# A fused conv–joint forward and backward kernel: first-chunk tanh rows by DMA transpose, SyncE's queue in source order, and the second chunk's x tiles moved up

## The chip, the cores and the metric

The kernel runs on one core of a Trainium2 chip. The metric is the device time of one execution in microseconds (us); lower is better. The kernel before took 866.32 us in the median of three runs (863.22 to 870.09).

## What is computed

The reference is the forward pass below and its gradients to all seven inputs for a given `grad_out`, all in bf16. B = 2, T = 16000, D = 256, three taps, U = 8.

```python
def _fwd_reference(x, w1, w2, g, w_f, w_g, w_o):
    h = sum over 3 taps of xp[:, i:i+T, :] @ w1[i]      # conv over time
    h = gelu(h)[:, ::2, :]                               # stride 2
    f = sum over 3 taps of hp[:, i:i+T1, :] @ w2[i]
    f = gelu(f)[:, ::2, :]                               # stride 2: 4000 rows
    fe = f @ w_f
    ge = g @ w_g
    j = tanh(fe[:, :, None, :] + ge[:, None, :, :])      # [2, 4000, 8, 256]
    return j @ w_o
```

The outputs are the result `out_0` [2, 4000, 8, 256] and the gradients of x, w1, w2, g, w_f, w_g and w_o. The bulk of the data is `grad_out` (read) and `out_0` (written).

## The kernel before

**Tiling.** The 4000 output rows of each batch are cut into 8 chunks of 512 rows (the last has 416), so there are 16 chunks, numbered n = 0 to 15. In a chunk the 8 values of u are taken in 4 pairs `up`. One pair is one *step*: a gradient part `gj` (L529), forward blocks `o_block` (L629), and the weight gradient `gwo` (L675) of the pair before.

**What runs beside what.** The main loop (L773) runs the pairs of chunk n (`joint_units`, L613, cut into short units by `yield`) and, woven between them by `weave` (L692), a *fill*: the convolutions of chunk n+1 (`conv_units` L227, `conv2_units` L264, `fe_units` L293), and the backward convolutions of chunk n−1. `ratio` (L800) is the number of fill units per main unit. Chunk 0 has no chunk before it, so its fill holds only the convolutions of chunk 1 and six empty units. The gelu pieces are queued and issued by `pump` (L194), one or two per main unit.

**x, grad_out and tanh tiles.** `load_x` (L130) brings one of four phases of x transposed into a tile XC (6 buffers) by a DMA transpose, `load_got` (L141) brings `grad_out` transposed (GOT, 6 buffers), `load_go` (L147) brings it as rows (GO, 3 buffers). The last chunk of each batch has 32 rows over; for these `load_go` brings four small pieces (GOs, 1 buffer, L158). All are issued on SyncE's queue (SP).

**JR: the tanh rows.** `tanh` (L307) writes JT with the channel on the partitions. The weight gradient `gwo` needs the same values with the row on the partitions, the tile JR (3 buffers). For n > 0, `load_jr` (L563) makes them by four DMA transposes per pair on SP (L574), issued in `ahead` (L811), after the tanh of the next pair. For n == 0 `load_jr` returns after it has allocated the tile (L569), and `joint_units` calls `jr_block` for each of the four 128-row blocks (L622–625): four transposes on TensorE into PSUM (L392) and one VectorE copy out of PSUM (L394).

**What sets the order.** The program is written in one order, but the framework's scheduler orders each engine's instructions itself: the source's order is a priority, and an instruction that the scheduler's own timing takes to be ready goes ahead. This holds for SP's queue also. Each queue is then executed in the order so fixed. Weights W2, WF, WO are loaded on SP at L709–711. The first loads after those are written at L760–766: two GOT, GO of pair 0, two GOT, and then the four x tiles of chunk 1. In each step (L801–809) the source loads one x tile of chunk n+2, GO of the next pair and two GOT tiles; then come the units of the pair, with `ahead` among them.

Of the kernel before, what the change touches and what calls it, by code (L numbers as in the profile page):

```python
# [22 lines left out]
P = 128  # L23
# [9 lines left out]
def kernel(  # L33
# [22 lines left out]
    nc = tc.nc  # L56
# [4 lines left out]
    G = len(chunks)  # L61
    xq = x.rearrange("b (q four) d -> b four q d", four=4)

    def geom(n):
        b, ci = chunks[n]
        c0 = ci * CW
        return b, ci, c0, min(CW, MQ - c0)

    def blocks(w):
        return [(o, min(P, w - o)) for o in range(0, w, P)]  # L70
# [59 lines left out]
    def load_x(n, c):  # L130
        b, ci, c0, W = geom(n)
        t = xcp.tile([P, KT, CW + 16], BF16, name="XC")
        if c == 3 and ci > 0:
            nc.sync.dma_start_transpose(out=t[:, :, 0:W + 16], in_=xq[b, c, c0 - 16:c0 + W, :])
        else:
            if c == 3:
                nc.vector.memset(t[:, :, 0:16], 0.0)
            nc.sync.dma_start_transpose(out=t[:, :, 16:16 + W], in_=xq[b, c, c0:c0 + W, :])
        S[n]["X", c] = t

    def load_got(n, u):  # L141
        b, ci, c0, W = geom(n)
        t = gotp.tile([P, KT, CW], BF16, name="GOT")
        nc.sync.dma_start_transpose(out=t[:, :, 0:W], in_=grad_out[b, c0:c0 + W, u, :])
        S[n]["GOT", u] = t

    def load_go(n, up):  # L147
        b, ci, c0, W = geom(n)
        t = gop.tile([P, 4, 2 * V], BF16, name="GO")
        nfull = W // P  # L150
        src = grad_out[b, c0:c0 + nfull * P, 2 * up:2 * up + 2, :]
        nc.sync.dma_start(out=t[:, 0:nfull, :], in_=src.rearrange("(tb p) u v -> p tb (u v)", p=P))
        S[n]["GO", up] = t
        r = W - nfull * P
        if r and up % 2 == 0:
            t = tailp.tile([P, V], BF16, name="GOs")
            for i in range(4):
                nc.sync.dma_start(out=t[i * r:(i + 1) * r, :], in_=grad_out[b, c0 + nfull * P:c0 + W, 2 * up + i, :])  # L158
            S[n]["GOs", up // 2] = t


# [367 lines left out]
    def gj(n, u):  # L529
        b, ci, c0, W = geom(n)  # L530
        st = S[n]
        JT, GOT = st["JT", u], st["GOT", u]
        JSQ = jsp.tile([P, KT, CW], BF16, name="JSQ")
        nc.scalar.activation(out=JSQ[:, :, :W], in_=JT[:, :, :W], func=ACT.Square)  # L534
        NGZ = ngzp.tile([P, KT, CW], BF16, name="NGZ")
        st["NGZ", u] = NGZ
        for mt in range(KT):
            ps = ps_f32()
            for kt in range(KT):
                nc.tensor.matmul(ps[:, :W], lhsT=WOT[:, kt, mt * P:(mt + 1) * P], rhs=GOT[:, kt, :W],  # L540
                                 start=(kt == 0), stop=(kt == KT - 1))
            nc.vector.scalar_tensor_tensor(out=NGZ[:, mt, :W], in0=JSQ[:, mt, :W], scalar=1.0, in1=ps[:, :W],  # L542
                                           op0=ALU.subtract, op1=ALU.mult,
                                           accum_out=NGGEc[:, b, mt, u, ci:ci + 1])
            yield
# [17 lines left out]
    def load_jr(n, up):  # L563

        W = geom(n)[3]
        nfull = W // P
        JR = jrp.tile([P, 4, 2, KT, P], BF16, name="JR")
        S[n]["JR", up] = JR
        if n == 0:  # L569
            return  # L570
        for j in range(2):
            JT = S[n]["JT", 2 * up + j]
            for kt in range(KT):
                nc.sync.dma_start_transpose(out=JR[:, 0:nfull, j, kt, :], in_=JT[:, kt, 0:nfull * P])  # L574
# [38 lines left out]
    def joint_units(n, up, ahead):  # L613
        b, ci, c0, W = geom(n)
        st = S[n]
        bl = blocks(W)[:W // P]
        us = (2 * up, 2 * up + 1)
        for u in us:
            yield from gj(n, u)
            ngfe_acc(n, u)  # L620
            short_jt(n, u)
        if n == 0:  # L622
            for k in range(len(bl)):
                jr_block(n, up, k)
                yield
        OUT = outp.tile([P, 4, 2 * V], BF16, name="OUT")
        JR = st["JR", up]

        def o_block(k):  # L629
            o, M = bl[k]  # L630
            ps = ps_f32()
            for j, u in enumerate(us):
                for kt in range(KT):
                    nc.tensor.matmul(ps[:M, j * V:(j + 1) * V], lhsT=st["JT", u][:, kt, o:o + M], rhs=WO[:, kt, :],  # L634
                                     start=(kt == 0), stop=(kt == KT - 1))
            nc.scalar.copy(out=OUT[:M, k, :], in_=ps[:M, :])  # L636

        ahead()
        pend = prev_gwo[0]
        o_block(0)  # L640
        yield
        o_block(1)
        yield
        if pend is not None:
            gwo(*pend, 0)
        yield
        if pend is not None:
            gwo(*pend, 1)
        yield
        for k in range(2, len(bl)):  # L650
            o_block(k)
            yield
            if pend is not None:
                gwo(*pend, k)
        yield
        if pend is not None:
            gwo_rest(*pend, len(bl))
        yield
        if W % P and up % 2:
            yield from short_block(n, up // 2)  # L660
        prev_gwo[0] = (n, up)
        nfull = W // P
        nc.gpsimd.dma_start(out=out_0[b, c0:c0 + nfull * P, us[0]:us[1] + 1, :].rearrange("(tb p) u v -> p tb (u v)", p=P),  # L663
                            in_=OUT[:, 0:nfull, :])
# [27 lines left out]
    def weave(main, fill, ratio):  # L692

        due = 0.0
        for _ in main:
            pump(2 if later else 1)
            due += ratio
            while due >= 1.0:
                due -= 1.0
                if next(fill, StopIteration) is StopIteration:  # L700
                    due = -1e9

    make_identity(nc, ident[:])
    nc.gpsimd.dma_start(out=W1[:], in_=w1.rearrange("i (kt p) n -> p i kt n", p=P))
    for c in (1, 0, 3, 2):
# [53 lines left out]

    for i in range(2):  # L760
        load_got(*order[i])
    load_go(*orderp[0])
    for i in range(2, 4):
        load_got(*order[i])
    for c in (1, 0, 3, 2):
        load_x(1, c)
    for _ in chain(warm(16), small_units(), conv_units(0), transposed_units(), warm(4), conv2_units(0), warm(16), fe_units(0)):
        pass
    for u in range(2):
# [3 lines left out]
    for n in range(G):  # L773
        back, fwd = n > 0, n + 1 < G
        conv = conv_units(n + 1) if fwd else iter(())
        parts = []
        if back:
            for (o, M) in blocks(window(n - 1)[1] - window(n - 1)[0]):
                load_x5(n - 1, o, M)
            d1, e, gwf = d1_units(n - 1), e_units(n - 1), gwf_units(n - 1)  # L780
            nfn = (len(blocks(geom(n - 1)[3])) + 1) // 2
            d5, gw2 = d5_units(n - 1), gw2_units(n - 1)
            nhg = len(blocks(geom(n - 1)[3]))
            parts += [islice(conv, 2), islice(d1, 1), islice(conv, 1), d1, conv,
                      islice(gwf, 1), islice(d5, 1), islice(gwf, nfn - 1), islice(d5, 1), islice(gw2, 1),
                      islice(d5, 1), islice(gw2, 1), d5, islice(gw2, nhg - 2), gwf, gw2]
        else:
            parts += [conv, iter([None] * 3)]
        if fwd:
            parts.append(conv2_units(n + 1))  # L790
        if back:
            parts.append(islice(e, 6))
        else:
            parts.append(iter([None] * 3))
        if fwd:
            parts.append(fe_units(n + 1))
        if back:
            parts.append(e)
        fill = chain(*parts)
        ratio = (0.85 if n > 0 else 0.28) if n + 1 < G else 0.72  # L800
        for up in range(U // 2):  # L801
            step = n * (U // 2) + up
            if n + 2 < G:
                load_x(n + 2, (1, 0, 3, 2)[up])
            if step + 1 < len(orderp):
                load_go(*orderp[step + 1])
            for i in range(2):
                if 2 * step + 4 + i < len(order):
                    load_got(*order[2 * step + 4 + i])

            def ahead():  # L811
                for i in range(2):
                    if 2 * step + 2 + i < len(order):
                        tanh(*order[2 * step + 2 + i])
                if step + 1 < len(orderp):
                    load_jr(*orderp[step + 1])

            weave(joint_units(n, up, ahead), fill, ratio)
            if up == U // 2 - 1:
                for _ in fill:  # L820
                    pump(2)
                pump(len(later) + len(lazy))
                lazy_on[0] = False
# [35 lines left out]
    n = G - 1  # L859
# [35 lines left out]
```

## Time and profile before

| what | us |
|---|---|
| median of 3 runs | 866.32 |
| the profiled execution, its own time | 865.56 |
| its span in the profile | 863.8 |
| TensorE (PE) busy | 831.3 |
| ScalarE (ACT) busy | 684.2 |
| VectorE (DVE) busy | 602.2 |
| GpSimd (POOL) busy | 407.2 |

The granted TensorE clock of this execution is 0.997 of full. PE's busy time includes overlap between pipelined matmuls. SP does no arithmetic; it only issues DMAs. A row of a table by windows gives a stretch of the span, its length, and the busy time of each engine in it; "x16" is a number of instructions. In the chain of waits each piece has its start, its length and what it was. "A <- B" names a wait of A that ended with B.

### The profile page before, as it was taken

How to read it: one execution, taken by the hardware profiler on the slowest of the kernel's cores; microseconds unless marked ns; L12 is line 12 of the kernel's file. 1: busy time of each engine (PE TensorE's matmuls, PEld its weight loads, DVE VectorE, ACT ScalarE, POOL GpSimd, SP SyncE). 2: the span in 40 equal slices, each digit the busy share in tenths (PEclk: the TensorE clock that was granted, in tenths of full speed). 3: DMA queues.
4: the chain of work that ended last, by engine and by line, in shares of the span. 5: the costliest groups of instructions: out<-in, count | busy, mean ns of one | idle time of the engine just before them, and what ended most of it. 6: DMA issues, size and time to landing. Idle time of an engine off the chain costs nothing.

```text
span 863.8 us, 17772 instructions
## 1 busy us (share of the span) xinstructions
PE 831.3 (96%) x6648; PEld 599.3 (69%) x6648; DVE 602.2 (70%) x1190; ACT 684.2 (79%) x1064; POOL 407.2 (47%) x452
## 2 busy tenths in 40 slices
PE   7878999999999999999999999999999999999998
PEld 3455777767767677777856677776776767777876
DVE  4697958759495784949678495875948669495552
ACT  4788897886969869696996969879696886969634
POOL 1255554535544444554453554543553535545750
PEclk9999999999999999999999999999999999999999
DMA  9999999999999999999899999999999999997952
GB/s 188 188 198 187 174 239 224 222 266 203 259 226 224 206 222 252 199 226 246 192 212 218 219 218 231 234 224 265 192 249 229 221 259 184 223 223 180 225 160 90
DMA packets 382612, 185.66 MB, mean 215 GB/s; under 512 B 330114, under 2 KB 366235, under 8 KB 382526
## 3 DMA queue, kind: packets, MB, share of 16 engines
q1 hardware_dynamic: 362878, 115.20, 76.7%
q0 software_dynamic: 19648, 69.32, 26.6%
q8 instruction: 52, 0.85, 0.4%
q14 instruction: 34, 0.28, 0.2%
HBM read 54.43 MB, written 50.34 MB: 121 GB/s over the span
## 4 chain that ended last, share of the span: by engine, by line
PE 53%; DVE 29%; ACT 13%; issue 2%; DMA 2%; POOL 0%; ACTq 0%; POOLq 0%; DVEq 0%
PE ps L512 8%; PE GWO_ps L683 7%; PE ps L246 7%; PE ps L489 7%; PE ps L540 7%; PE ps L634 6%; DVE NGZ L542 6%; DVE G L199 5%; DVE g_sq L199 5%; DVE g_s L197 4%; DVE GH L381 3%; PE pst L392 3%; ACT JSQ L534 3%; PE ps L378 3%; ACT JT L312 2%
## 5 line engine op out<-in xcount | busy, mean ns | idle before, releaser
L561 POOL TENSOR_TENSOR ACCN<-ACCN,NGZ 128x1024 f32<-128x1024 f32 (+1 forms) x80 | 170.3, 2129 | 126.6 <-DVE NGZ L542 124.1
L542 DVE SCALAR_TENSOR_TENSOR NGZ<-JSQ,ps 128x512 bf16<-128x512 bf16 (+1 forms) x256 | 163.4, 669 | 83.6 <-ACT GX L492 47.7
L534 ACT ACTIVATE JSQ<-JT 128x1024 bf16<-128x1024 bf16 (+1 forms) x128 | 135.3, 1061 | 86.6 <-DVE NGZ L542 86.6
L312 ACT ACTIVATE JT<-FE,GE 128x512 bf16<-128x512 f32 (+1 forms) x256 | 171.2, 737 | 0.1
L636 ACT CAST OUT<-ps 128x512 bf16<-128x512 f32 x248 | 147.7, 614 | 3.8 <-PE ps L634 3.3
L634 PE MATMUL ps<-WO,JT 128*128 128x256 bf16 x992 | 148.1, 272 | 0.9 <-DVE NGZ L542 0.5
L683 PE MATMUL GWO_ps<-GO,JR 128*128 128x256 bf16 x992 | 140.2, 273 | 0.0
L540 PE MATMUL ps<-GOT,WOT 128*128 128x512 bf16 (+1 forms) x512 | 138.4, 374 | 1.8 <-DVE JR L394 1.1
L197 DVE SCALAR_TENSOR_TENSOR g_s<-g_sq,g_x 128x1024 bf16<-128x1024 bf16 (+1 forms) x45 | 74.7, 1659 | 58.5 <-ACT g_sq L197 58.5
L634 PEld LDWEIGHTS <-JT 128*128 128x128 bf16 x992 | 94.5, 98 | 24.9 <-issue 1.4
L683 PEld LDWEIGHTS <-JR 128*128 128x128 bf16 x992 | 95.3, 98 | 18.3 <-issue 1.1
L489 PE MATMUL ps<-W1T,GH 128*128 128x256 bf16 (+2 forms) x768 | 104.2, 273 | 0.0
L512 PE MATMUL ps<-rows,X 128*128 128x256 bf16 (+2 forms) x768 | 94.2, 272 | 8.1 <-DVE rows L394 8.1
L331 DVE TENSOR_TENSOR ACC<-ACC,ps 128x512 f32<-128x512 f32 x84 | 55.4, 680 | 57.4 <-PE ps L512 56.3
L246 PE MATMUL ps<-XC,W 128*128 128x512 bf16 (+1 forms) x384 | 91.9, 376 | 2.7 <-DMA XC<-in_x_dram 2.4
L512 PEld LDWEIGHTS <-X 128*128 128x128 bf16 (+2 forms) x768 | 74.5, 98 | 23.1 <-issue 11.5
L663 POOL DMA_DIRECT2D out_dram<-OUT x64 | 49.4, 772 | 86.8 <-ACT OUT L636 84.4
L492 ACT CAST GX<-ps 128x512 bf16<-128x512 f32 (+2 forms) x128 | 74.3, 592 | 15.0 <-PE ps L489 11.6
L489 PEld LDWEIGHTS <-GH 128*128 128x128 bf16 (+2 forms) x768 | 75.0, 99 | 15.6 <-issue 1.4
L540 PEld LDWEIGHTS <-WOT 128*128 128x128 bf16 x512 | 49.1, 98 | 43.9 <-issue 2.6
L502 POOL DMA_DIRECT2D out_dram<-GX x60 | 33.6, 559 | 70.1 <-ACT GX L492 64.1
L246 PEld LDWEIGHTS <-W 128*128 128x128 bf16 x384 | 37.7, 98 | 40.7 <-issue 4.4
(139 smaller groups left out, 1289.3 us busy)
## 6 DMA issues: line engine op xcount, KB each, us to landing
GO<-in_grad_out_dram SPq DMA_DIRECT2D x56, 512.0 KB, 5.2
out_dram<-OUT POOLq DMA_DIRECT2D x56, 512.0 KB, 5.4
X<-in_x_dram POOLq DMA_DIRECT2D x58, 320.0 KB, 7.6
out_dram<-GX POOLq DMA_DIRECT2D x55, 256.0 KB, 4.1
JR<-JT SPq DMA_TRANSPOSE x240, 4.9
GO<-in_grad_out_dram SPq DMA_DIRECT2D x8, 384.0 KB, 3.9
out_dram<-OUT POOLq DMA_DIRECT2D x8, 384.0 KB, 4.7
GOT<-in_grad_out_dram SPq DMA_TRANSPOSE x128, 5.2
```

Of the source, the lines that this page charges most:

```text
L197: later.popleft()()
L246: nc.tensor.matmul(ps[:, :W], lhsT=W1[:, i, kt, mt * P:(mt + 1) * P], rhs=st["X", c][:, kt, 16 + sh:16 + sh + W], start=(k == 0), stop=(k ...
L312: nc.scalar.activation(out=JT[:, mt, :W], in_=S[n]["FE"][:, mt, :W], func=ACT.Tanh, bias=GE[:, b, mt, u:u + 1], scale=1.0)
L489: nc.tensor.matmul(ps[:Mx, cj * D:(cj + 1) * D], lhsT=GH[:, par, kt, j:j + Mx], rhs=W1T[:, i, kt, :], start=(k == 0), stop=(k == last))
L512: nc.tensor.matmul(ps[:, dt * D:(dt + 1) * D], lhsT=st["X5", o][:M, i + 2 * par, dt * P:(dt + 1) * P], rhs=t[:M, j + 2 * par:j + 2 * par + ...
L534: nc.scalar.activation(out=JSQ[:, :, :W], in_=JT[:, :, :W], func=ACT.Square)
L540: nc.tensor.matmul(ps[:, :W], lhsT=WOT[:, kt, mt * P:(mt + 1) * P], rhs=GOT[:, kt, :W], start=(kt == 0), stop=(kt == KT - 1))
L542: nc.vector.scalar_tensor_tensor(out=NGZ[:, mt, :W], in0=JSQ[:, mt, :W], scalar=1.0, in1=ps[:, :W], op0=ALU.subtract, op1=ALU.mult, accum_ ...
L561: nc.gpsimd.tensor_tensor(out=out, in0=in0, in1=st["NGZ", u][:, :, :W], op=ALU.add)
L634: nc.tensor.matmul(ps[:M, j * V:(j + 1) * V], lhsT=st["JT", u][:, kt, o:o + M], rhs=WO[:, kt, :], start=(kt == 0), stop=(kt == KT - 1))
L636: nc.scalar.copy(out=OUT[:M, k, :], in_=ps[:M, :])
L683: nc.tensor.matmul(GWO_ps[:, dt, :], lhsT=JR[:M, k, j, dt, :], rhs=GO[:M, k, j * V:(j + 1) * V], start=(n_gwo[0] == 0), stop=(n_gwo[0] == ...
```

## The change

1. `load_jr` returns early, and `joint_units` calls `jr_block`, only for (n, up) = (0, 0). Pairs 1 to 3 of chunk 0 get their JR by four DMA transposes each on SP, as the later chunks do.
2. A `manual_schedule` region over SP is opened before the first instruction: from there to the end SP issues in the order of the source. The other engines are still ordered by the scheduler.
3. Of chunk 1's x tiles, phases 1, 0 and 3 are written ahead of GO of pair 0, and phase 2 right after it, ahead of the GOT tiles 2 and 3.
4. The four small GOs loads, four times in the kernel, go to GpSimd's queue.
5. `ratio` of chunk 0 is 0.36 in place of 0.28. Chunk 0 then has 52 main units (16, 12, 12, 12), where it had 64.

```diff
@@ -155,7 +155,7 @@
             for i in range(4):
-                nc.sync.dma_start(out=t[i * r:(i + 1) * r, :], in_=grad_out[b, c0 + nfull * P:c0 + W, 2 * up + i, :])
+                nc.gpsimd.dma_start(out=t[i * r:(i + 1) * r, :], in_=grad_out[b, c0 + nfull * P:c0 + W, 2 * up + i, :])
@@ -566,7 +566,7 @@
         S[n]["JR", up] = JR
-        if n == 0:
+        if (n, up) == (0, 0):
             return
@@ -619,7 +619,7 @@
             short_jt(n, u)
-        if n == 0:
+        if (n, up) == (0, 0):
             for k in range(len(bl)):
                 jr_block(n, up, k)
                 yield
@@ -700,6 +700,7 @@
+    ctx.enter_context(tc.manual_schedule(engines={mybir.EngineType.SP}))
     make_identity(nc, ident[:])
@@ -759,11 +760,12 @@
     for i in range(2):
         load_got(*order[i])
+    for c in (1, 0, 3):
+        load_x(1, c)
     load_go(*orderp[0])
+    load_x(1, 2)
     for i in range(2, 4):
         load_got(*order[i])
-    for c in (1, 0, 3, 2):
-        load_x(1, c)
@@ -797,7 +799,7 @@
-        ratio = (0.85 if n > 0 else 0.28) if n + 1 < G else 0.72
+        ratio = (0.85 if n > 0 else 0.36) if n + 1 < G else 0.72
```

## The prediction

> **What bounds the kernel now.** I read the page first, for the bound over the span, then a table of windows cut at the chunks, because the change acts in one chunk.
>
> ```profile
> PE 831.3 (96%) x6648; PEld 599.3 (69%) x6648; DVE 602.2 (70%) x1190; ACT 684.2 (79%) x1064; POOL 407.2 (47%) x452
> ```
>
> TensorE is busy 96%; 863.8 − 831.3 = 32.5 us of idle is all that can be won without removing PE work. The windows say where it lies:
>
> ```profile
> 26.60:72.50 45.90, 35.86 (x253) 22.62 (x252) 38.94 (x83) 39.77 (x61) 23.19 (x16) 0.96 0.89 186
> 176.50:228.50 52.00, 50.82 (x408) 36.91 (x406) 36.70 (x70) 42.61 (x67) 25.05 (x26) 1.00 1.08 234
> 228.50:280.50 52.00, 50.82 (x408) 36.95 (x407) 36.94 (x70) 42.62 (x67) 25.06 (x26) 1.00 1.08 233
> ```
>
> The columns are the stretch, its length, then PE, weight loads, DVE, ACT and POOL busy, granted clock, DMA share, GB/s. A later chunk takes 52.0 us and idles PE 1.2 of them: it is bound by PE. Chunk 0 (26.6 to 72.5, from its first joint matmul to the first convolution matmul issued in chunk 1) idles PE 10.0 of 45.9 us. There DVE has 38.9 us and ACT 39.8: no engine is full, and the end is set by a chain through all three. The chain of waits, in order of time, names its pieces (start, length, what):
>
> ```profile
> 26.58 5.17 DMA XC<-in_x_dram
> ...
> 43.90 0.34 DVE JR L394
> ...
> 48.82 0.99 DVE JR L394 x3
> ...
> 57.20 1.33 DVE JR L394 x4
> 58.53 2.50 DVE g_sq L199
> ...
> 64.56 0.61 DVE FT L197
> ...
> 72.12 0.34 DVE JR L394
> ```
>
> So one x tile and the JR copies of chunk 0's pairs 1 to 3 stand in the chain that leads to FT, to fe and to chunk 1. PE's own waits (who waited, on whom: total us, times, longest) say how much of the x transfer was a stall:
>
> ```profile
> PE ps L302 <- DVE FT L197: 3.0, 1, 3.0
> PE ps L246 <- DMA XC<-in_x_dram: 2.4, 1, 2.4
> PE ps L279 <- DVE JR L394: 1.2, 1, 1.2
> PE ps L540 <- DVE JR L394: 1.1, 1, 1.1
> ```
>
> **The change part by part.** The sum is made against the profiled execution, 865.56 us (span 863.8, 1.76 around it); the median of the runs is 0.76 above it.
>
> *JR by DMA for three pairs.* Removed: 48 TensorE transposes. Eight in a row take 0.45 us in the chain, 56 ns each: 2.7 us of PE. Removed too: 12 PSUM copies on DVE; the 16 of the window take 5.68 us, 0.355 each, 4.26 for twelve. On the chain lie 0.34 + 0.99 + 1.33 before FT and 0.34 at 72.12: 3.0 us. I credit 3.0 us. The other 1.26 us lie beside ACT or PE work, as the 2.7 us on PE do, since PE idles 10 us in that chunk.
>
> Added: 12 DMA transposes on SP, median 1.24 us of issue each, 14.9 us, and 4.9 us median to landing (longest 13.8). Nothing on a compute engine. The first waits for the tanh of u = 3, which ended at 38.3. Behind it on SP then wait the x, GO and two GOT loads of the next step. Pair 1's rows are needed where its first gwo stands, at 50.5 in the trace; 38.3 + 4 × 1.24 + 4.9 = 48.2. I take 0, and bound it above with the longest rows: four such transposes took up to 8.91 us in a later chunk; 38.3 + 8.91 + 4.9 = 52.1, late by 1.6 us a pair; three pairs, 4.8 us. A gain from the wait itself is excluded: it only adds a condition.
>
> *x tiles of chunk 1 early.* Before, phase 3 was issued at 26.58 and landed at 31.75, and PE stood 2.4 us. By the order of the source, SP issues two GOT until 13.40, then phases 1, 0, 3. XC has 6 buffers: four hold chunk 0, one the zero tile, so phase 0 waits for a buffer until chunk 0's convolution ends (its last matmuls end at 15.1). Three issues at 1.25 us each bring phase 3 to about 17.6, and landing, 5.2 to 11.4 us, to 23 to 29; it is wanted at 29.4. The wait goes: −2.4 us. GO of pair 0 moves behind three transposes, 13.4 to about 18; its first use is at 33.5. GOT of u = 2 and 3 moves to about 19 to 22; first use 41.2. Both cost 0.
>
> *SP in source order.* It moves every DMA of SP for 16 chunks, so this is the unknown. A later step in source order is x, GO, two GOT, then four JR behind their tanh. Before, it was GO and four JR with the GOT around them, and the x tiles of a chunk nearly in one row (192.8 to 199.9 for chunk 3). Issue per step: 1.25 + 0.53 + 2 × 1.29 + 4 × 1.24 = 9.3 us of a 13.0 us step. Waits for buffers: GO of step s+1 takes that of s−2, read until the end of step s−1, so free; GOT's was read at the start of step s−1; x phase 3 of chunk n+2 takes a tile of n+1 whose convolution ran in pair 0. What is late next is the last x tile, issued in step 3, some 10 us or more before use, against 5.1 us to landing. PE shows no DMA wait after chunk 0 in the whole list. So 0, bounded below by the 1.2 us idle of each later chunk (DVE waits, which a DMA queue hardly touches) and above by the rival below.
>
> *GOs on POOL.* 16 issues of 0.42 us leave SP, and 16 at 0.56 to 0.77 us (POOL's issue rows) come to an engine with 25 of 52 us busy: up to 12 us, in four places. What queues behind them is POOL's ACCN adds, and behind these NGFE. POOL idles on DVE for 134 us before those adds; I take 0, and at most 4 × 0.77 = 3.1 us for each of two places in which it stands ahead of NGFE: +6. *ratio 0.36:* 14 fill units end at main unit 39 of 52 instead of 50 of 64, both close to the start of pair 3, so conv2 and fe stay in place within two or three units: 0; before it ends, 12 JR units are gone from the mix.
>
> Sum: −3.0 − 2.4 = −5.4 us. 865.56 − 5.4 = 860.2; on the scale of the median 866.32 − 5.4 = 860.9. I predict 861. The cap: if chunk 0 came down to its PE work, 35.9 − 2.7 = 33.2 us, it would save 12.7 us; down to ACT's 39.8 us, 6.1.
>
> **Rivals.** *Chunk 0 tightens past the chain.* With the PSUM banks free earlier, the PE waits after FT on DVE and JR (0.5 + 0.3 + 1.1 + 0.3 = 2.2 us) and FT's own 3.0 go also: up to 5.4 + 5.2 = 10.6, and not beyond 12.7: 856 to 853.6. For: those waits name JR copies. Against: ACT is 87% busy there and its work stays, so this needs ACT's evictions to slide into chunk 1, where ACT already has 47.3 of 51.7 us.
>
> *Only the x wait goes.* ACT's order takes the place of the DVE copies (DVE waits 4.3 us on ACT's g_sq at 36.5): −2.4, 864.
>
> *The rows come late.* The bound above: −5.4 + 4.8 = −0.6, 865.7; with one landing of 13.8 us, 38.3 + 8.91 + 13.8 − 50.5 = 10.5 late once: 871. For: DMA share is 0.89 already in that window. Against: later chunks carry the same rows with a share of 1.08 and PE waits on none. The Trainium skill, VectorE: DVE Perf Modes, sections "The three transpose paths" and "Rules for kernel authors", speaks against the change: it gives 390 ns for a 128×128 block by TensorE, 1309 ns by DMA, and advises TensorE if PSUM can be the destination. By its figures an estimate for the 48 blocks is 63 us against 19, and the sum would come out slower by up to 44 us if both lay on the path. The trace disagrees on the size: 56 ns a block on PE in a row, and 1.24 us of SP for four blocks.
>
> *SP's order starves the steps (slower).* In source order JR of the next pair blocks all later loads. The place is each step of chunks 1 to 15. If four JR always took the longest group, 8.91 us, a step would need 8.91 + 4.36 = 13.3 us of SP against 13.0 of PE: 0.3 us a step, 60 steps, 18 us: 866.3 + 18 − 5.4 = 879. It decides at 13.0 us. Against: the four groups from 176 to 228 take 8.91, 7.14, 7.00 and 5.73, mean 7.2, and 11.6 with the rest.
>
> **How the numbers follow.** The forecast, 0.45 (its own range 858 to 864). Tightens, 0.17. Only x, 0.10. Rows late, 0.10. SP starves, 0.18. A change of 1% (8.7 us) is about what a measurement can tell from none: faster means under 857.7, slower over 875.0. Faster: the 0.17 and 0.03 of the forecast's low edge, 0.20. Slower: the 0.18 and 0.02 for two late places at once, 0.20. The same: 0.60. The range from 853.6 to 873 leaves out most of the SP case, 0.18.
>
> **What would show it.** Right: no PE wait on XC near 29; phase 3 issued before 20; no JR copies after 36; 12 JR transposes on SP between 36 and 65; FT some 5 us earlier, the first convolution in chunk 1 near 67; later chunks 52.0 with 50.8 busy. Wrong: gwo L683 waiting on JR in chunk 0 (rows late); PE waits on GOT, XC or JR in later chunks and chunks over 52.3 (SP); the first convolution at 70 with ACT full (only x), or before 63 (tightens); POOL waiting at L158 ahead of NGFE.

## The result, and the profile after

The kernel after took 933.11 us in the median of six runs (918.61 to 956.26), the kernel before 866.2 us in six (863.22 to 870.09). The ratio is 1.0653, with a 95% interval of 1.0599 to 1.0707: slower, where 861 us and no measurable change were forecast. The medians here and below are over all runs, while a ratio leaves out runs more than 1.5% above the fastest of their kernel (here the three longest), so it can be smaller than that of the medians. The profiled execution after took 927.83 us, its span is 926.1 us, its granted clock 0.963.

From the page of the kernel after, the busy times of the engines, and the shares of the chain that ended last:

```profile
PE 839.6 (91%) x6527; PEld 602.9 (65%) x6600; DVE 597.0 (64%) x1178; ACT 686.5 (74%) x1064; POOL 411.7 (44%) x468
PE 43%; ACT 21%; DMA 17%; DVE 14%; issue 3%; SPq 1%; POOL 0%; another core or an unknown queue 0%; ACTq 0%; POOLq 0%; DVEq 0%
```

The span grew by 926.1 − 863.8 = 62.3 us. TensorE is busy 8.3 us longer (839.6 against 831.3) and idle 86.5 us where it was idle 32.5: 54.0 us of the 62.3 are new idle time (some 70 matmuls are missing from the records of this trace, so a little of it may be work). The second line says with what: 17% of the chain is DMA, where it was 2% before. The list of PE's waits (who waited, on whom: total us, times, longest) names the transfers:

```profile
PE ps L540 <- DMA GOT<-in_grad_out_dram: 38.8, 11, 8.2
PE GWO_ps L683 <- DMA JR<-JT: 13.0, 4, 4.9
PE ps L246 <- DMA XC<-in_x_dram: 9.7, 1, 9.7
```

The three DMA waits are 61.5 us. The same list of the kernel before has one of them, 2.4 us on XC. So the loss is not where the prediction looked for the gain: most of the waiting is for GOT, in the later chunks. The windows of the kernel after (chunk 0, a slow chunk, a good chunk; columns as before) show it stage by stage:

```profile
28.30:74.50 46.20, 33.24 (x205) 19.91 (x207) 35.24 (x71) 36.11 (x56) 19.45 (x14) 0.89 0.88 176
178.90:240.60 61.70, 52.67 (x405) 37.90 (x409) 36.73 (x71) 43.48 (x67) 24.51 (x26) 0.92 1.04 192
643.30:695.70 52.40, 50.80 (x405) 37.15 (x409) 36.96 (x71) 43.04 (x67) 25.08 (x26) 1.00 1.09 228
```

In chunk 0 the transposes left PE and DVE nearly as worked out: 33.2 and 35.2 us where they had 35.9 and 38.9. ACT's work in the window fell too, from 39.8 to 36.1, which was not worked out. But the chunk is not shorter (46.2 us against 45.9), and the clock there is 0.89. Chunk 3 takes 61.7 us and idles PE for 9.0; the good chunk takes 52.4, as most did before. The lengths of the chunks, read between the first convolutions:

| kernel | first convolution in chunk 1 at | chunks 1 to 13, us each |
|---|---|---|
| before | 72.5 | 51.5, 52.3, then 52.4 four times, 49.8, 48.0, 54.1, 51.2, 52.4 three times |
| after | 74.5 | 52.1, 52.3, 61.7, 60.2, 57.8, 57.5, 55.0, 53.5, 54.8, 63.9, 52.4 three times |

But for the first 2 us the loss begins in chunk 3, over 100 us after the last transpose that the change added.

**Why GOT is late.** The chain of waits after, around the longest wait (start, length, what):

```profile
180.57 2.92 SPq L144
...
183.54 19.02 DMA GOT<-in_grad_out_dram
...
202.61 0.61 PE ps L540
```

This GOT, the second of its step, took 19.0 us from issue to landing; the median is 5.8 us (5.2 before). The first, issued at 180.6, ended PE's longest wait only at 199.5. SP's timeline after (start, duration, line, what) shows what it was issued among:

```profile
178.60 1.29 SPq L138 DMA_TRANSPOSE XC<-in_x_dram  x1
179.99 0.53 SPq L152 DMA_DIRECT2D GO<-in_grad_out_dram  x1
180.57 9.83 SPq L144 DMA_TRANSPOSE GOT<-in_grad_out_dram  x2
190.50 12.23 SPq L574 DMA_TRANSPOSE JR<-JT  x4
202.78 2.59 SPq L138 DMA_TRANSPOSE XC<-in_x_dram  x1
```

And GpSimd's queue in the same place:

```profile
180.95 2.14 POOL L182 DMA_DIRECT2D X<-in_x_dram  x4
```

GO, two GOT, the four X5 loads of a new chunk (L182, 320 KB each) and one store of 512 KB (L663, at 180.2) are issued within 3.6 us. SP's timeline before, in the same chunk, has one GOT to each side of the JR:

```profile
178.72 1.89 SPq L144 DMA_TRANSPOSE GOT<-in_grad_out_dram  x1
180.70 0.77 SPq L152 DMA_DIRECT2D GO<-in_grad_out_dram  x1
181.56 8.91 SPq L574 DMA_TRANSPOSE JR<-JT  x4
190.91 1.79 SPq L144 DMA_TRANSPOSE GOT<-in_grad_out_dram  x1
```

The burst is regular, and the waits go with it. In the kernel after, X5 loads begin at 181, 243, 304, 361, 418 and 526; PE's waits of over 2 us for a GOT end at 200, 260, 319, 378, 434 and 540, each time 14 to 19 us later. Not every burst is followed by such a wait: those at 78, 129 and 472 and from 581 on are not.

**Why a late GOT is felt.** The kernel before has the same bursts (its longest GOT landing is 11.2 us) and no such wait, because there GOT is issued long before its use. From issue to the first use of the result on VectorE, mean of each chunk, chunks 0 to 15, in us:

| kernel | lead of GOT |
|---|---|
| before | 28 35 25 25 27 30 26 24 25 24 23 26 27 29 32 26 |
| after | 25 18 13 13 12 12 12 12 13 10 14 17 17 15 12 12 |

SP's own waits before, from 72.5 to 800 us, show what held that lead up (the issue of GOT, on the engine that still reads the buffer):

```profile
SPq L144 <- PE ps L540: 35.5, 22, 6.1
SPq L144 <- PE ps L634: 34.9, 31, 2.3
```

With the smaller groups of the same kind, 101 of the 112 GOT issues in that stretch waited for a free buffer, 134.9 us in all: SP asked for GOT as early as six buffers allow. After, the same list has two such waits:

```profile
SPq L144 <- PE ps L378: 7.3, 1, 7.3
SPq L144 <- PE ps L634: 2.5, 1, 2.5
```

So SP is behind: a buffer is free and the issue comes late. From landing to use, GOT had 11.5 us at the least before (22.3 median), and 0.8 after (6.0 median). The group of GOT's issues (ns: least, median, longest), before and then after, shows that issuing became slower too:

```profile
L144 SPq DMA_TRANSPOSE GOT<-in_grad_out_dram x128: 1223/1304/6202, 10.3 to 806.8; - x128
```

```profile
L144 SPq DMA_TRANSPOSE GOT<-in_grad_out_dram x128: 1215/2082/7562, 10.4 to 876.1; - x128
```

**What a wait costs besides.** After such a wait PE is slow for a moment. PE's timeline after:

```profile
199.51 1.89 PE L540 MATMUL ps<-GOT,WOT 128*128 128x512 bf16 x4 [8.24 <-DMA GOT<-in_grad_out_dram]
```

Four matmuls took 1.89 us; four of the same line took 1.03 at 682.8, in a chunk without waits. This is where the 8.3 us more of busy time come from, at least in part: the slow chunk's window has a clock of 0.92 and 52.7 us busy, the good one 1.00 and 50.8. The Trainium skill, TensorE: Matmul & The Clock Gate, section "What's actually happening", says that the array's clock falls to half after an idle window of some 3.4 us and comes back after as long a busy one. The trace agrees: nearly twice the time, behind a wait of 8.2 us, and a granted clock of 0.50 from 194.2 to 204.5, from 2.9 us after PE stopped to 5.0 us after it went on.

### The profile page after: what moved, and what is told of

It is laid out like the page before. It is cut to its first block, busy times and chain, and to the rows that moved or that the text cites. A ratio compares the mean times of both kernels' runs of the same rounds, so it can differ in the third digit from the quotient of the medians.

```text
span 926.1 us, 17456 instructions
## 1 busy us (share of the span) xinstructions
PE 839.6 (91%) x6527; PEld 602.9 (65%) x6600; DVE 597.0 (64%) x1178; ACT 686.5 (74%) x1064; POOL 411.7 (44%) x468
## 3 DMA queue, kind: packets, MB, share of 16 engines
HBM read 54.43 MB, written 50.34 MB: 113 GB/s over the span
## 4 chain that ended last, share of the span: by engine, by line
PE 43%; ACT 21%; DMA 17%; DVE 14%; issue 3%; SPq 1%; POOL 0%; another core or an unknown queue 0%; ACTq 0%; POOLq 0%; DVEq 0%
DMA GOT<-in_grad_out_dram 12%; ACT JT L312 7%; PE ps L512 6%; PE ps L489 6%; PE GWO_ps L683 6%; PE ps L540 5%; PE ps L634 5%; DMA JR<-JT 4%; ACT JSQ L534 3%; ACT OUT L636 3%; PE pst L392 3%; DVE g_s L197 3%; PE ps L448 3%; DVE NGZ L542 2%; ACT g_sq L197 2%
## 5 line engine op out<-in xcount | busy, mean ns | idle before, releaser
L312 ACT ACTIVATE JT<-FE,GE 128x512 bf16<-128x512 f32 (+1 forms) x256 | 171.0, 738 | 10.6 <-DMA JR<-JT 10.5
L540 PE MATMUL ps<-GOT,WOT 128*128 128x512 bf16 (+1 forms) x474 | 140.6, 388 | 41.2 <-DMA GOT<-in_grad_out_dram 38.8
L683 PE MATMUL GWO_ps<-GO,JR 128*128 128x256 bf16 x992 | 142.5, 276 | 13.3 <-DMA JR<-JT 13.0
L540 PEld LDWEIGHTS <-WOT 128*128 128x128 bf16 x512 | 49.6, 100 | 86.5 <-DMA GOT<-in_grad_out_dram 42.0
L394 ACT COPY rows<-pst 128x1024 bf16<-128x1024 bf16 x64 | 63.3, 1021 | 50.8 <-PE pst L392 50.8
L663 POOL DMA_DIRECT2D out_dram<-OUT x64 | 49.6, 776 | 93.4 <-ACT OUT L636 91.5
L512 PEld LDWEIGHTS <-X 128*128 128x128 bf16 (+2 forms) x768 | 74.5, 98 | 17.9 <-issue 6.2
```

The source lines that it names most:

```text
L312: nc.scalar.activation(out=JT[:, mt, :W], in_=S[n]["FE"][:, mt, :W], func=ACT.Tanh, bias=GE[:, b, mt, u:u + 1], scale=1.0)
L512: nc.tensor.matmul(ps[:, dt * D:(dt + 1) * D], lhsT=st["X5", o][:M, i + 2 * par, dt * P:(dt + 1) * P], rhs=t[:M, j + 2 * par:j + 2 * par + ...
L683: nc.tensor.matmul(GWO_ps[:, dt, :], lhsT=JR[:M, k, j, dt, :], rhs=GO[:M, k, j * V:(j + 1) * V], start=(n_gwo[0] == 0), stop=(n_gwo[0] == ...
```

## The experiments

The expectations name the theories by letters. A: the order of SP's queue is the cause by itself. B: the transposes added to chunk 0 cost SP its lead, which it never wins back. C, formed after the first four: the source's order packs GO and two GOT together, where they slow each other's issue and meet X5. The rivals to C were that any fixed order of SP does this, or that SP's DMAs in that number are too slow in themselves. Ratios are to runs of the kernel before on the same chip, with 95% intervals.

### 1. The order alone

```diff
 # before
+    ctx.enter_context(tc.manual_schedule(engines={mybir.EngineType.SP}))
     make_identity(nc, ident[:])
```

> The kernel before with one line added: SP issues in source order; nothing else of the change. Theory A (order): source order fixes the queue as x, GO, two GOT, four JR a step, so that the HBM reads GO and GOT of the step at a chunk's start are issued with the four X5 loads of GpSimd's queue, land 15 us and more later, and gj waits: 900 to 950 us, PE waits on GOT of 4 to 10 us once a chunk. Theory B (lost lead): the twelve added JR transposes take SP some 15 us in chunk 0 that it never makes up; without them the order costs little: 862 to 872, no PE wait on GOT.

939.4 us, ratio 1.0817 (1.072 to 1.0914). PE's waits:

```profile
PE ps L540 <- DMA GOT<-in_grad_out_dram: 37.4, 10, 7.3
PE ps L246 <- DMA XC<-in_x_dram: 11.6, 4, 6.6
PE GWO_ps L683 <- DMA JR<-JT: 7.2, 4, 4.5
```

One line makes the whole loss, and the same GOT waits. The lead falls from 25 us to 8 by chunk 7, and not one issue of GOT between 72.5 and 800 us waits for a buffer. Chunk 0 is better, though: its first convolution comes at 69.2 (72.5 before), since in the source's order the x tiles go out early without being moved in the source.

### 2. The added transposes alone

```diff
 # before
-        if n == 0:
+        if (n, up) == (0, 0):      # in load_jr and in joint_units
-        ratio = ... 0.28
+        ratio = ... 0.36
```

> The kernel before with JR by DMA for pairs 1 to 3 of chunk 0 (and ratio 0.36, without which the text order of fe and tanh breaks); SP in the scheduler's order, x tiles where they were. Theory A (order): the recorded sum's JR part, 3 us less, 858 to 868, later chunks 52 us. Theory B (lost lead): slow as the whole change, 890 to 950, with PE waits on GOT or JR in later chunks.

874.16 us, ratio 1.0097 (1.0063 to 1.0132). From PE's waits, which name no GOT:

```profile
PE GWO_ps L683 <- DMA JR<-JT: 8.8, 6, 3.9
...
PE ps L246 <- DMA XC<-in_x_dram: 3.4, 1, 3.4
```

With the order free there is no GOT wait, so B has no ground. But the rows come late: the first convolution moves to 79.2, and the clock of chunk 0 (26.6 to 79.2) is 0.81. This part of the change costs some 8.5 us where a gain of 3.0 was credited, so the time lies in the range of neither theory.

### 3. All of the change but the order

```diff
 # after
-    ctx.enter_context(tc.manual_schedule(engines={mybir.EngineType.SP}))
```

> The changed kernel without the region that keeps SP in source order; all else of the change stays. Theory A (order): back to 855 to 868, no PE wait on GOT in later chunks. Theory B (lost lead): 890 to 950.

869.31 us, ratio 1.0041 (1.0008 to 1.0074). Without the one line the loss is gone, though the time lies 1.3 us above theory A's range; what is left is again JR: PE waits 14.8 us on it, 10 times, and on no GOT.

### 4. The change with chunk 0's rows by TensorE

```diff
 # after
-        if (n, up) == (0, 0):      # in load_jr and in joint_units
+        if n == 0:
-        ratio = ... 0.36
+        ratio = ... 0.28
```

> The changed kernel with the rows of chunk 0 again made by TensorE (and ratio 0.28 with them); source order, early x tiles and GOs on GpSimd stay. Theory A (order): still slow, 900 to 950, with the GOT waits. Theory B (lost lead): 860 to 870, no GOT waits.

914.95 us, ratio 1.0559 (1.0477 to 1.0641). By theory B the time would be near that of the kernel before, so theory B falls. PE waits as with the change:

```profile
PE ps L540 <- DMA GOT<-in_grad_out_dram: 35.1, 10, 7.4
PE ps L246 <- DMA XC<-in_x_dram: 15.4, 5, 5.7
```

It is faster than experiment 1, whose interval lies wholly above. The two differ in the place of the x loads and in the queue of GOs; in experiment 1 SP stands twice, 18.1 us in all, behind a GOs (L158), for whose single buffer it waits. Which of the two makes the difference was not separated. All six GOT waits of over 2 us here end 13 to 19 us after the start of an X5 burst, as with the change; in experiment 1 five of seven do, after 14 to 20 us.

### 5 and 6. The same fixed order, with the loads between the JR

The loads of a step are kept back and one is issued after each of the four JR transposes: still a fixed order, with as many DMAs. In 6 chunk 0's rows come by TensorE, as in 4.

```diff
 # after (5), experiment 4 (6)
                 nc.sync.dma_start_transpose(...)          # JR, L574
+                if loads:
+                    loads.popleft()()
...
-                load_x(n + 2, (1, 0, 3, 2)[up])
+                loads.append(partial(load_x, n + 2, (1, 0, 3, 2)[up]))   # GO and both GOT likewise
...
+                while loads:                              # in ahead, behind load_jr
+                    loads.popleft()()
```

> The changed kernel, SP still in source order, but the source's order within a step altered: the x, GO and two GOT loads are written between the four JR transposes (JR, x, JR, GO, JR, GOT, JR, GOT) instead of ahead of them; same instructions, same bytes. Theory C (packing): four HBM reads in a row back up the queue and SP stands in the second GOT, four JR in a row leave transfer time unused; taken in turn a chunk needs some 48 us of SP as before the change, the lead of GOT holds near 20 us, 855 to 872, no PE wait on GOT. Rival (any fixed order): SP in one fixed order blocks behind the JR's wait for tanh and behind GO's buffer whatever the order in a step: 900 to 950, GOT waits stay.

> The same order within a step, with all rows of chunk 0 made by TensorE as before the change (ratio 0.28). Theory C (packing): 858 to 866, chunk 0 ends some 3 us earlier than in the kernel before because the x wait is gone, later chunks 52 us. Rival (any fixed order): 900 to 940 as with the source order that groups the loads.

5: 879.84 us, ratio 1.0152 (1.0069 to 1.0235). 6: 877.42 us, ratio 1.0112 (1.0049 to 1.0175). A fixed order as such is not the cause: about four fifths of the loss are gone with the order still fixed. The upper end of C's range for 5 was passed by 8 us, and 6 missed its 866. GOT's issue comes back:

```profile
L144 SPq DMA_TRANSPOSE GOT<-in_grad_out_dram x128: 1234/1408/5985, 9.6 to 829.2; - x128
```

That is 1.41 us in the median (1.30 before, 2.08 after); the mean between 72.5 and 800 us is 1.92 (2.40 after), so it comes back in part. The lead of GOT recovers only in part: 7 and 12 us in chunks 1 and 2, then 14 to 19; PE still waits 12.1 us on GOT in 5, of which 8.0 at 145. Order within the step is thus most of the cause. The edit does two things that these runs don't separate: it puts JR between the loads, and it moves GOT away from the X5 loads. The rows of chunk 0 make no difference here that the intervals can tell (5 against 6).

### 7. SP's queue by itself

The kernel leaves out all computation and the outputs. SP issues the loads of 24 steps four times over: packed, in turn with the JR, packed, in turn. Stores were meant to go with the last two.

> SP's queue by itself: four stages of 24 steps, each step one x, one GO, two GOT and four JR of the kernel's sizes, from a constant tile; no TensorE, ScalarE or gradient work and no outputs but the stores of stages 3 and 4 (one 512 KB store per step on GpSimd's queue). Stages 1 and 3 issue x, GO, GOT, GOT, then four JR; stages 2 and 4 in turn. Theory C (packing): a step takes 11 to 13 us in stage 1 with the second GOT at 2 to 3 us, and at least 1 us less in stage 2; with the stores both grow and the gap stays. Rival (fixed cost per DMA): stages 1 and 2 take the same, some 10 us a step.

One step of the third stage, packed (SP's timeline):

```profile
711.43 1.30 SPq L130 DMA_TRANSPOSE XC<-in_x_dram  x1
712.78 0.58 SPq L130 DMA_DIRECT2D GO<-in_grad_out_dram  x1
713.40 4.41 SPq L130 DMA_TRANSPOSE GOT<-in_grad_out_dram  x2
717.86 5.21 SPq L130 DMA_TRANSPOSE JR<-JTc  x4
723.11 1.30 SPq L130 DMA_TRANSPOSE XC<-in_x_dram  x1
```

And one of the second stage, in turn:

```profile
469.24 1.30 SPq L130 DMA_TRANSPOSE XC<-in_x_dram  x1
470.59 1.27 SPq L130 DMA_TRANSPOSE JR<-JTc  x1
471.90 0.58 SPq L130 DMA_DIRECT2D GO<-in_grad_out_dram  x1
472.52 1.19 SPq L130 DMA_TRANSPOSE JR<-JTc  x1
473.76 1.30 SPq L130 DMA_TRANSPOSE GOT<-in_grad_out_dram  x1
475.10 1.26 SPq L130 DMA_TRANSPOSE JR<-JTc  x1
476.41 1.30 SPq L130 DMA_TRANSPOSE GOT<-in_grad_out_dram  x1
...
479.06 1.30 SPq L130 DMA_TRANSPOSE XC<-in_x_dram  x1
```

No engine computes, so nothing but the transfers is there to wait for, and yet the two GOT take 4.4 us when they follow GO, 2 × 1.30 when JR stand between. In the mean of a stage a step takes 11.23 us packed and 9.88 to 9.91 in turn. So packing costs 1.3 us a step with nothing else on the way. GpSimd ran its stores ahead: all 48 had landed by 90 us, when the first two steps of the first stage were just over. These two took 21 and 67 us, the other 22 of that stage 11.4 in the mean. What stores at the kernel's pace do to either order was therefore not measured.

### 8. The change without the X5 burst

X5 is loaded for two chunks only, and the w1 gradient of the later ones is computed from the second one's tiles.

```diff
 # after
+            if n <= 2:
                 load_x5(...)
+            S[n - 1]["X5", o] = S[min(n - 1, 1)]["X5", o]
...                                       # the last chunk likewise
```

> The changed kernel, with the x rows of the backward pass (X5, four loads of 320 KB a chunk on GpSimd's queue) loaded for chunks 0 and 1 only and chunk 1's tiles used for all later ones, so the gradient of w1 is left out in effect; SP's queue is unaltered. Theory C with the X5 burst as the trigger: without the burst SP, at some 11.2 us a grouped step when alone, keeps its lead and the GOT waits go: 868 to 885. Rival (SP's grouped order is too slow by itself beside the stores): the lead still falls by some 2 us a chunk and the GOT waits of 4 to 8 us stay: 900 to 940.

875.42 us, ratio 1.0108 (1.0042 to 1.0175), in C's range. The first PE waits:

```profile
PE GWO_ps L683 <- DMA JR<-JT: 8.1, 3, 4.5
PE ps L512 <- DVE rows L394: 7.8, 12, 0.8
```

No GOT wait is left, though the order is that of the change, GOT's issue is as slow (median 2.06 us), and the lead falls as low (10 us in chunk 6; it is 20 at the end). The burst is what makes the small lead hurt. It also takes 17.9 MB of HBM reads away (36.57 MB on its page against 54.43), so it doesn't show by itself that the burst's place, and not its volume, matters; the distance of 14 to 19 us from burst to wait speaks for the place. The profiled execution is the fastest of four (868.5 us, the others 872 to 879).

### 9 and 10. The other half: more lead, with the burst

As 5 and 6, and GOT is written one step earlier in the source (six before the loop in place of four).

```diff
 # experiment 5 (9), experiment 6 (10)
-                    loads.append(partial(load_got, *order[2 * step + 4 + i]))
+                    loads.append(partial(load_got, *order[2 * step + 6 + i]))
...
-    for i in range(2, 4):
+    for i in range(2, 6):
         load_got(*order[i])
```

> The changed kernel with the loads in turn with JR, and the GOT tiles loaded one step earlier in the source (six before the loop, then those of step s+3 in step s; same six buffers). The lead of GOT grows by one step of 13 us. If the rest of the loss with the loads in turn is the small lead of GOT in chunks 0 to 2, PE waits on GOT go and the time is 864 to 872; what is left is gwo's wait on JR in chunk 0, some 5 to 8 us. If it is something else (the JR's wait for tanh holding x and GO), 875 to 882.

> The same, with chunk 0's rows all by TensorE (ratio 0.28): no wait on GOT, no wait on JR in chunk 0, and the x wait of the kernel before gone: 859 to 865, some 3 us under the kernel before. If x or GO behind the JR's wait become late instead, 870 to 878.

9: 880.32 us, ratio 1.0103 (1.005 to 1.0156). 10: 878.24 us, ratio 1.0137 (1.0077 to 1.0197). The lead did what was expected: in 9 it is 18 to 25 us, 107 GOT issues wait for a buffer again, and PE waits on no GOT in either. The time did not follow: it is that of 5 and 6. PE's waits in 9:

```profile
PE GWO_ps L685 <- DMA JR<-JT: 9.8, 5, 4.8
...
PE ps L246 <- DMA XC<-in_x_dram: 5.6, 3, 3.6
```

GOT now waits on SP for its buffer, 173.8 us in all, and the x tile and JR stand behind it in the fixed order; 10 has one x wait of 10.5 us. Both times missed the first range that was named for them. 880.32 lies in the second one of 9, by which something else is left (what stands behind JR's wait for tanh), and 878.24 is 0.2 us above that of 10; the x waits speak for it, without showing it. Both stay open in part: the profiled run of 9 took 868.7 us, most of its other runs 878 to 887, and what these do differently has no trace.

### 11. The x part alone

```diff
 # before
-    idle = xcp.tile([P, KT, CW + 16], BF16, name="XC")
+    idle = outp.tile([P, 4, 2 * V], BF16, name="OUT")
...
+    for c in (1, 0, 3, 2):
+        load_x(1, c)
     load_go(*orderp[0])
     for i in range(2, 4):
         load_got(*order[i])
-    for c in (1, 0, 3, 2):
-        load_x(1, c)
```

> The kernel before, SP in the scheduler's order, with chunk 1's x tiles written ahead of GO and the zero tile of the warm-up taken from OUT's pool, so that one more x buffer is free and phase 3 is issued some 3 us earlier: the x wait of 2.4 us alone goes. The recorded sum's x part: 2.4 us less, 862 to 865. If the wait is given back later in chunk 0, 865 to 867.

863.2 us, ratio 0.9954 (0.9923 to 0.9986): some 4 us under the kernel before, a small gain, but the interval does not hold 1. The zero tile of the warm-up no longer holds an x buffer, which the change itself did not do; phases 1 and 0 go out from 12.8 on, and phase 3 at 23.7 (26.6 before). The first convolution comes at 69.2 (72.5 before), and the list of PE's waits up to 72 us has no XC; the longest is now

```profile
PE ps L302 <- DVE FT L197: 3.0, 1, 3.0
```

## Why the prediction was wrong

**The bound: right.** TensorE bounds the later chunks, 52.0 us with 50.8 busy. That was read as safety; it also means that every new wait of PE there goes straight into the time.

**JR by DMA: wrong, by some 11 us** (8.5 lost and 3.0 not won). The step that failed is "I take 0" for the landing of JR. The work left PE and DVE as worked out, and experiment 2 still lost 8.5 us where 3.0 were credited. The sum looked at pair 1 alone (ready at 48.2, wanted at 50.5; counted by 16 gwo matmuls a pair, its first stood at 47.4). Nearly all the waiting came behind the later transposes of the chunk, whose landing the sum never worked out: experiment 2 has it from 59.8 to 71.2 (and 0.7 us at 48.3), the kernel after from 63 to 67, 8.2 us in the window of chunk 0. The sum also took PE's order to stay. Pair 3's first gwo matmuls stood at 79.0 before, behind fe (L302). After, the scheduler has three of them right ahead of fe, at the time at which their rows are still being issued (60.6 to 66.3). PE's timeline before, and after:

```profile
78.99 1.04 PE L683 MATMUL GWO_ps<-GO,JR 128*128 128x256 bf16 x8
```

```profile
63.12 0.40 PE L683 MATMUL GWO_ps<-GO,JR 128*128 128x256 bf16 x1 [4.93 <-DMA JR<-JT]
65.03 0.39 PE L683 MATMUL GWO_ps<-GO,JR 128*128 128x256 bf16 x1 [1.51 <-DMA JR<-JT]
67.16 0.40 PE L683 MATMUL GWO_ps<-GO,JR 128*128 128x256 bf16 x1 [1.73 <-DMA JR<-JT]
67.34 0.63 PE L302 MATMUL ps<-FT,WF 128*128 128x512 bf16 x1
```

At their old place these three would not have waited, since the rows that they need were there by 67.2; no run tested that by itself. In the windows with these waits the granted clock is lower as well (0.81 and 0.89, against 0.96 before). The "rows come late" rival held the mechanism, and its two prices (4.8 and 10.5 us late) hold the 8.2 between them. The Trainium skill, VectorE: DVE Perf Modes, section "Rules for kernel authors", advised TensorE for such blocks; experiment 2 agrees with its direction, 5 against 6 shows no difference. The runs don't agree with the size that its figures gave (up to 44 us): what counted was not the time of the transposes but when their rows landed and where they were wanted.

**x tiles early: right.** −2.4 us was forecast, experiment 11 won some 4 (1.2 to 6.7 by its interval), with one more x buffer than the change has. In the kernel after, phase 3 is issued at 16.5 and the XC wait is gone from chunk 0. The first convolution of experiment 11, at 69.2, is 3.3 us earlier.

**SP in source order: wrong, and this decided it.** The step that failed is "So 0". Three readings led there.
- *"Issue per step 9.3 us of a 13.0 us step"* took each row's length from the old order and carried it over to the new. For issuing alone in the old order 9.3 was about right, although the means of the rows between 72.5 and 800 us give 12.0 us a step (1.62 us for JR, 1.63 GOT, 1.58 x, 0.65 GO): much of these means is waiting inside the rows. GOT's rows exceed 1.25 us each by 42 us in all, and 38 of these lie in rows in which a wait ended less than 0.9 us before the row did. After, the means are 1.56, 2.40, 1.79 and 0.62, 13.45 us a step. GOT's rows now exceed 1.25 us by 117 us, and only 8 of these lie in rows with such a wait. So the order itself made a GOT dearer to issue, as experiment 7 shows for the queue alone, and the sum took that cost as fixed.
- *"The last x tile, issued some 10 us or more before use"* compared the lead with one landing of 5.1 us, and GOT's lead wasn't compared at all. It was 25 us, against landings up to 11.2; the source's order left 12, against landings up to 19.0.
- *"PE shows no DMA wait after chunk 0"* is a fact about the old order. It held there with a lead of 25 us, and the lead was what the change gave up.

**The SP rival: right place, wrong price.** It had a chance of 0.18 and 879 us. Its condition came true (13.45 us of SP's rows a step, against 13.0), but through GOT, whose mean issue grew from 1.63 to 2.40 us, and not through JR, which stayed. It priced the deficit of the queue alone, 18 us. What a late load costs is decided by its landing beside the burst, up to 8.2 us a time, and by the clock behind the wait; so the loss was over three times as large.

**GOs on POOL and ratio:** neither was run alone. POOL's busy time rose by 4.5 us. Experiment 4 beats experiment 1 with GOs on POOL, so no cost shows, though the earlier x loads could hide a small one.

**The range** ended at 873 and so left out most of the SP case. Its chance of 0.18 was low for a rival whose own row had 11.6 us of SP in a step of 13.0.

**What is shown and what is argued.** Shown: the order alone makes the loss (1, 3); the added transposes don't (4); the order within a step is most of it (5, 6), and packing makes the same DMAs slower to issue (7); without the burst, or with the loads in turn and the lead restored, no GOT wait is left (8; 9 and 10). Argued only: why a second GOT behind GO is issued more slowly, that the burst's place and not its volume counts, and why SP loses its lead in experiment 8 too, at 12.2 us a step. Open: how much of the gain of 5 and 6 is the spacing and how much the distance from the burst, and the last 1% of experiments 5, 6, 9 and 10.

## What to carry to other kernels

Before the order of a DMA queue is fixed by hand, tabulate the lead of each load (issue to first use) and what holds it: loads that wait for a buffer are as early as they can be, and an order in which they no longer wait has spent that reserve. Compare the lead with the longest landing, not the median. Before the rows of a queue are added up to its load, take the waits inside them out, and don't carry a row's length from one order to another. Within a step of a queue like this one, put transposes that read from SBUF between the loads that read from HBM, and try to keep the loads away from the place where another queue starts a burst. When a result is made another way, ask also where the scheduler will now place its use.

## What the runs showed of the hardware

- The order of the same eight DMAs changed what SP needs to issue them: 11.23 us with the loads packed, 9.90 in turn with transposes of an SBUF tile (experiment 7). The second of two GOT behind GO took 2.25 to 3.14 us in the third stage; with JR between them either one took 1.3 in the median.
- A transpose of 256 KB from HBM landed after 19.0 us beside GO, another GOT and, on GpSimd's queue, four loads of 320 KB and a store of 512 KB; its median is 5.8 us. The X5 loads suffered too: their longest landing went from 12.7 us to 17.8.
- A wait of PE for 8.2 us was followed by four matmuls in 1.89 us in place of 1.03: here a stall cost more than its own length.
